# Seven products of halves in an order that changes the PSUM bank, and at the start one weight piece loaded earlier and one prepared later

## The chip, the cores and the metric

The kernel runs on one core of one Trainium2 chip. The metric is the device time of one execution in microseconds; lower is better. The kernel before takes 654.24 us (median of 4 runs, 654.07 to 654.77). Its profiled execution has a span of 652.4 us; in all profiled executions here the time is 1.7 to 2.0 us above the span.

## The reference

```python
# attention: B=4, H=8, S=768, D=48
for t in range(S):
    cur = einsum('bhd,bhe->bhde', u * k_t, v_t)
    y[:, :, t] = einsum('bhd,bhde->bhe', r_t, state + cur)
    state = w_t[..., None] * state + einsum('bhd,bhe->bhde', k_t, v_t)
x = y.transpose(0, 2, 1, 3).reshape(3072, 384)
# MLP: w_in is 384 x 2048, w_out is 2048 x 384
h = x @ w_in
g = 0.5 * h * (1 + erf(h / sqrt(2)))
out = g @ w_out
```

The two weights arrive as 64-bit floats and are converted to 32-bit floats on the chip.

## The kernel before

The tokens are worked on in eight stretches x = 0 to 7 of 384. Each needs an attention and an MLP, and the MLP of x - 1 runs interleaved with the attention of x: the MLP is a generator that is advanced step by step, and at chosen steps one attention "slot" is put in. The last MLP, x = 7, has no attention beside it.

For x > 0 two of the three blocks of 128 tokens of the second MLP product are done with seven products of half size in place of eight (sums of blocks in, sums of results out). Each product is 16 matmuls 128x192. They accumulate in two PSUM tiles of one bank each, o1/o3 in one bank (A), o2 in the other (B):

```python
o1, o2 = psum(), psum()                       # tag "mm", two buffers
product(o1, of_blocks(0, 0), of_w(0, 0), True)
nc.scalar.copy(out=p1, in_=o1)                # P1, bank A, ScalarE reads
yield
product(o1, of_blocks(0, 1), of_w(1, 0))
nc.scalar.copy(out=o_sb[0][:, 0:HM], in_=o1)  # P2, bank A
yield
product(o2, of_sums(s2), of_t(1), True)
nc.vector.tensor_add(u2, o2, p1)              # P3, bank B, VectorE reads
yield
product(o2, of_sums(s3), of_t(2))
nc.vector.tensor_add(u3, o2, p1)              # P4, bank B
for k in range(2):
    nc.vector.tensor_sub(s2[k], gs[k + 2][:, :, 0:128], s2[k])
yield
o3 = psum()
product(o3, of_sums(s1), of_t(0), True)
nc.vector.tensor_add(o_sb[1][:, HM:], o3, u3) # P5, bank A
yield
product(o2, of_blocks(1, 1), of_t(3))
nc.vector.tensor_add(o_sb[1][:, 0:HM], o2, p1)# P6, bank B
...                                           # store of o_sb[1]
yield
product(o3, of_sums(s2), of_w(1, 1))
nc.vector.tensor_add(o_sb[0][:, HM:], o3, u2) # P7, bank A
...                                           # store of o_sb[0]
```

A weight piece (16 in all) is loaded by SyncE's queue into a raw buffer, made into f and e by ScalarE (`prepare`), and into the 32-bit weight by four VectorE operations (`finish`). `conversion` of piece i first prepares piece i + 1, then finishes piece i, then loads piece i + 3:

```python
def conversion():
    i = converted[0]
    ...
    prepare(i + HALFWAY)                      # HALFWAY = 2
    if wide:
        yield from finish(pieces[i][0], raws[i], *halfway[i])
    for _ in weight_in():
        pass
```

The start, up to the first MLP, at the end of the attention of x = 0 (it runs as two units):

```python
for _ in chain(shares, weight_in(), weight_in()):  # last share of x=1, v; second and third piece
    pass
convert()                       # first piece
for unit in units[:-1]: ...     # y of one unit: ysb, its transfers, two ScalarE copies into xT
for _ in range(2): ...
piece = conversion()            # second piece; prepares the third on ScalarE
next(piece)
next(units[-1])                 # y of the other unit: two VectorE and two ScalarE copies into xT
for _ in piece:
    pass
slots = attention(1, 0)
next(slots)
keep_warm(12)                   # twelve matmuls on zeros
```

## Time and profile before

| | before |
|---|---|
| median of 4 runs | 654.24 us |
| span of the profiled run | 652.4 us |
| TensorE, VectorE, ScalarE busy | 97%, 59%, 28% |
| first MLP matmul begins | 49.53 us |
| first update of r for x = 1 (VectorE) begins | 60.87 us |
| period of the MLP blocks x = 1 to 6 | 75.4 to 75.6 us |
| waits of the products for u2 | 7 of 0.8 us |

TensorE is the bound: from about 125 us on the chain of work that ended last is only matmuls. The prediction below shows the lines on the products and on the start. One more place is needed, the time-ordered records between the first MLP matmul and the first update of r. The columns are start, duration, engine, line, operation, output and inputs, shapes, count, and in brackets the idle time before it with what ended it.

```profile
57.27 1.61 PE L315 MATMUL d<-kx,rkw_in 64*64 64x64 f32 x92
...
60.51 0.33 PE L315 MATMUL d<-kx,rkw_in 64*64 64x64 f32 x4 [1.63 <-issue]
...
60.87 1.76 DVE L350 TENSOR_TENSOR rkw_in<-rkw_in 128x1536 f32<-128x1536 f32 x1 [4.47 <-PE d L315]
```

In a group of 96 equal matmuls TensorE stops for 1.63 us after the 92nd, waiting for nothing that the profile shows ("issue"); VectorE's update of r needs the end of that group.

### The profile page before, as it was taken

How to read it: one execution, taken by the hardware profiler on the slowest of the kernel's cores; microseconds unless marked ns; L12 is line 12 of the kernel's file. 1: busy time of each engine (PE TensorE's matmuls, PEld its weight loads, DVE VectorE, ACT ScalarE, POOL GpSimd, SP SyncE). 2: the span in 40 equal slices, each digit the busy share in tenths (PEclk: the TensorE clock that was granted, in tenths of full speed). 3: DMA queues.
4: the chain of work that ended last, by engine and by line, in shares of the span. 5: the costliest groups of instructions: out<-in, count | busy, mean ns of one | idle time of the engine just before them, and what ended most of it. 6: DMA issues, size and time to landing. Idle time of an engine off the chain costs nothing.

```text
span 652.4 us, 17509 instructions
## 1 busy us (share of the span) xinstructions
PE 633.8 (97%) x7937; PEld 451.2 (69%) x7937; DVE 382.6 (59%) x718; ACT 183.9 (28%) x338; POOL 5.7 (1%) x20
## 2 busy tenths in 40 slices
PE   8898998999999999999999999999999999999997
PEld 4555665566796668866697667966688667975695
DVE  8977999756941676428761479426763378600120
ACT  2245465233302531043212432024311432122200
POOL 3000000000000000000000000000000000000000
PEclk9999999999999999999999999999999999999999
DMA  4576347115001340004101240013301000010000
GB/s 169 157 248 242 103 157 267 34 47 139 12 3 36 82 113 2 26 22 126 58 2 35 66 131 2 11 37 86 99 2 34 15 1 2 2 35 13 0 1 36
DMA packets 20409, 43.26 MB, mean 66 GB/s; under 512 B 2672, under 2 KB 6512, under 8 KB 20336
## 3 DMA queue, kind: packets, MB, share of 16 engines
q1 hardware_dynamic: 13344, 26.97, 12.1%
q10 hardware_dynamic: 6992, 15.18, 8.7%
q8 instruction: 62, 1.02, 0.6%
q14 instruction: 11, 0.09, 0.0%
HBM read 36.24 MB, written 4.72 MB: 63 GB/s over the span
## 4 chain that ended last, share of the span: by engine, by line
PE 85%; DVE 9%; issue 2%; ACT 1%; DMA 1%; ACTq 0%; SPq 0%; DVEq 0%
PE h_ps L566 35%; PE o_ps L584 20%; PE o_ps L638 14%; PE d L401 6%; PE d L315 3%; DVE rkw_in L350 2%; PE y_ps L485 2%; PE y_ps L503 2%; DVE e L264 1%; PE kv_ps L453 1%; DVE a_sb L358 1%; DMA raw<-in_w_in_dram 1%; PE kt_ps L437 1%; PE warm L167 1%; DVE w_out_sb L268 1%
## 5 line engine op out<-in xcount | busy, mean ns | idle before, releaser
L566 PE MATMUL h_ps<-xT,w_in_sb 128*128 128x384 f32 x768 | 257.4, 490 | 1.1 <-ACT xT L516 1.1
L566 PEld LDWEIGHTS h_ps<-xT,w_in_sb 128*128 128x128 f32 x768 | 143.3, 190 | 97.7 <-ACT xT L516 1.5
L568 ACT ACTIVATE g<-h_ps 128x384 f32<-128x384 f32 x128 | 62.9, 491 | 210.5 <-PE h_ps L566 210.4
L638 PE MATMUL o_ps<-w_out_sb,g 128*128 128x384 f32 x320 | 106.2, 489 | 0.0
L638 PEld LDWEIGHTS o_ps<-w_out_sb,g 128*128 128x128 f32 x320 | 59.9, 190 | 40.4 <-DVE o_sb L644 0.6
L425 DVE COPY_PREDICATED a_sb<-quarter,d 128x384 f32<-128x384 uint8 x162 | 82.6, 552 | 3.7
L584 PE MATMUL o_ps<-t,s 128*128 128x192 f32 x336 | 58.2, 330 | 3.6 <-DVE u L612 3.6
L584 PEld LDWEIGHTS o_ps<-t,s 128*128 128x128 f32 x336 | 54.3, 190 | 6.0 <-DVE u L612 5.7
L644 DVE COPY o_sb<-o_ps 128x384 f32<-128x384 f32 x10 | 5.6, 558 | 87.1 <-PE o_ps L638 87.0
L401 PEld LDWEIGHTS d<-kx,rkw_in 64*64 64x64 f32 x1728 | 36.4, 133 | 9.8 <-issue 6.5
L401 PE MATMUL d<-kx,rkw_in 64*64 64x96 f32 x1728 | 39.8, 245 | 0.0
L519 ACT COPY ysb<-y_ps 128x384 f32<-128x384 f32 x8 | 3.8, 477 | 125.7 <-PE y_ps L503 125.7
L584 PE MATMUL o_ps<-w_out_sb,g 128*128 128x192 f32 x224 | 38.8, 327 | 0.4 <-ACT p L606 0.4
L584 PEld LDWEIGHTS o_ps<-w_out_sb,g 128*128 128x128 f32 x224 | 36.6, 190 | 2.6 <-ACT p L606 0.7
L380 ACT COPY kx<-rkw_in 128x384 f32<-128x384 f32 x54 | 31.2, 645 | 24.3 <-PE d L401 20.2
L412 DVE TENSOR_TENSOR rkw_in<-rkw_in,tot_sb 128x768 f32<-128x768 f32 x18 | 17.2, 957 | 31.7 <-PE d L401 31.7
L315 PEld LDWEIGHTS d<-rkw_in 64*64 64x64 f32 x1152 | 18.7, 134 | 11.9 <-issue 5.6
L576 DVE TENSOR_TENSOR s<-g 128x512 f32<-128x512 f32 x14 | 9.6, 686 | 28.9 <-ACT g L568 28.9
L167 PE MATMUL warm<-zeros 128*128 128x512 bf16 x81 | 23.2, 408 | 2.3 <-ACT zeros L162 2.3
L516 ACT COPY xT<-y_ps 48x384 f32<-48x384 f32 x46 | 21.8, 474 | 12.5 <-issue 12.0
L315 PE MATMUL d<-rkw_in 64*64 64x64 f32 (+1 forms) x1152 | 21.3, 221 | 3.0 <-issue 1.3
L612 DVE TENSOR_TENSOR u<-o_ps,p 128x192 f32<-128x192 f32 x7 | 2.5, 358 | 35.1 <-PE o_ps L584 35.1
(80 smaller groups left out, 569.6 us busy)
## 6 DMA issues: line engine op xcount, KB each, us to landing
rkw_in<-in_rkw_dram ACTq DMA_DIRECT2D x40, 288.0 KB, 2.9
raw<-in_w_out_dram SPq DMA_DIRECT2D x8, 768.0 KB, 4.4
raw<-in_w_in_dram SPq DMA_DIRECT2D x7, 768.0 KB, 7.9
rkw_in<-in_rkw_dram SPq DMA_DIRECT2D x16, 288.0 KB, 5.8
out_dram<-o_sb SPq DMA_DIRECT2D x24, 192.0 KB, 1.9
v_in<-in_v_dram ACTq DMA_DIRECT2D x5, 584.0 KB, 3.8
v_in<-in_v_dram SPq DMA_DIRECT2D x3, 584.0 KB, 6.6
rkw_in<-in_rkw_dram SPq DMA_DIRECT2D x2, 768.0 KB, 5.8
```

What stands on the lines that cost most here:

```text
L167: nc.tensor.matmul(t, lhsT=zeros[:, 0:128], rhs=zeros, start=True, stop=True)
L315: nc.tensor.matmul(d[half[p], g, n * width:(n + 1) * width], lhsT=kc[half[g], b, i, p], rhs=right(half[g], b, i, p), start=True, stop=True)
L350: nc.vector.tensor_mul(rk, rk, tt)
L380: nc.scalar.copy(out=z, in_=r4[:, :, :, f, :])
L401: nc.tensor.matmul(d[half[p], g, i * 3 * C // 2:(i + 1) * 3 * C // 2], lhsT=kc[half[g], (n + i) // NI, (n + i) % NI, p], rhs=rx[half[g], 2 ...
L412: nc.vector.tensor_mul(z, z, t2[:, :, 1:2].to_broadcast(z.shape))
L425: nc.vector.copy_predicated(out=an[:, :, :, :, (a + 1) * h:], mask=mask.to_broadcast(data.shape), data=data)
L516: copy(out=xT[s, pair, :].rearrange("p (i c t) -> p c i t", c=2, t=C), in_=y[s])
L566: nc.tensor.matmul(h_ps, lhsT=w_in_sb[:, f // FI, j, f % FI * 128:(f % FI + 1) * 128], rhs=xT[:, j, :], start=(j == 0), stop=(j == NJ - 1))
L568: nc.scalar.activation(out=gs[group][:, f % FG], in_=h_ps, func=AF.Gelu)
L584: nc.tensor.matmul(o, lhsT=lhs(j), rhs=rhs(j), start=start and j == 0, stop=(j == HF - 1), skip_group_check=True)
L638: nc.tensor.matmul(o, lhsT=block(i, f // HF, f % HF), rhs=w_out_sb[:, f, :], start=(f == 0), stop=(f == NF - 1))
```

## The change

It has two aims: no product should follow one in the same bank whose result is still being read, and ScalarE's last copies of x should not stand behind the preparation of a weight piece. For the latter, the second piece is also loaded ahead of the last share and v.

```diff
-    def conversion():
+    def conversion(ahead=True):
...
-        prepare(i + HALFWAY)
+        if ahead:
+            prepare(i + HALFWAY)
...
             product(o2, of_sums(s2), of_t(1), True)
             nc.vector.tensor_add(u2, o2, p1)
             yield
+            o3 = psum()
+            product(o3, of_sums(s1), of_t(0), True)
+            for k in range(2):
+
+                nc.vector.tensor_sub(s2[k], gs[k + 2][:, :, 0:128], s2[k])
+            yield
             product(o2, of_sums(s3), of_t(2))
             nc.vector.tensor_add(u3, o2, p1)
-            for k in range(2):
-
-                nc.vector.tensor_sub(s2[k], gs[k + 2][:, :, 0:128], s2[k])
-            yield
-            o3 = psum()
-            product(o3, of_sums(s1), of_t(0), True)
             nc.vector.tensor_add(o_sb[1][:, HM:], o3, u3)
             yield
             product(o2, of_blocks(1, 1), of_t(3))
...
-    for _ in chain(shares, weight_in(), weight_in()):
+    for _ in chain(weight_in(), shares, weight_in()):
         pass
...
-    piece = conversion()
+    piece = conversion(ahead=False)
     next(piece)
     next(units[-1])
     for _ in piece:
         pass
+    prepare(HALFWAY + 1)
```

More of the change, by code (lines that the diff above doesn't have):

```diff
@@ L613, in mlp @@
             yield
-            product(o2, of_sums(s3), of_t(2))
-            nc.vector.tensor_add(u3, o2, p1)
+            o3 = psum()
+            product(o3, of_sums(s1), of_t(0), True)
             for k in range(2):
@@ L619, in mlp @@
             yield
-            o3 = psum()
-            product(o3, of_sums(s1), of_t(0), True)
+            product(o2, of_sums(s3), of_t(2))
+            nc.vector.tensor_add(u3, o2, p1)
             nc.vector.tensor_add(o_sb[1][:, HM:], o3, u3)
```

## The prediction

> **What bounds the kernel now.** I read the busy table first, then the list of who waited for whom, then the time-ordered records around each edited place. I call the seven products of halves by their place in the kernel before: P1, P2 (bank A, read by ScalarE), P3 (bank B, read into u2), P4 (B, read into u3), P5 (A, o3), P6 (B), P7 (A).
>
> ```profile
> PE 633.8 (97%) x7937; PEld 451.2 (69%) x7937; DVE 382.6 (59%) x718; ACT 183.9 (28%) x338; POOL 5.7 (1%) x20
> ```
>
> TensorE is busy for 97% of a span of 652.4 us, and the chain that ended last is 85% TensorE. From about 125 us on that chain is nothing but matmuls, one block of about 75.4 us per x (210.46, 286.06, 361.43 start the same group). So a microsecond in which TensorE stands still is a microsecond of the run, and time saved on another engine there is worth nothing. The list of waits names such stills:
>
> ```profile
> PEld o_ps L584 <- DVE u L612: 5.7, 7, 0.8
> PE o_ps L584 <- DVE u L612: 3.6, 7, 0.5
> ```
>
> Seven times, once for each x that uses the halves, the products wait for VectorE's u2. The time-ordered records of the block for x = 1 (start, duration, engine, line, operation):
>
> ```profile
> 182.80 2.87 PE L584 MATMUL o_ps<-t,s 128*128 128x192 f32 x16
> 185.78 0.36 DVE L612 TENSOR_TENSOR u<-o_ps,p 128x192 f32<-128x192 f32 x1 [4.86 <-PE o_ps L584]
> ...
> 186.19 5.17 PEld L584 LDWEIGHTS o_ps<-t,s 128*128 128x128 f32 x32 [0.81 <-DVE u L612]
> 186.19 5.47 PE L584 MATMUL o_ps<-t,s 128*128 128x192 f32 x32 [0.52 <-DVE u L612]
> ...
> 190.28 0.42 DVE L470 TENSOR_TENSOR st<-st,kv_ps 128x96 f32<-128x96 f32 x2
> 190.61 0.35 DVE L615 TENSOR_TENSOR u<-o_ps,p 128x192 f32<-128x192 f32 x1
> 190.88 1.28 DVE L618 TENSOR_TENSOR s<-g,s 128x512 f32<-128x512 f32 x2
> 191.59 1.63 PE L485 MATMUL y_ps<-a_sb,v_in 64*64 64x64 f32 x96
> ...
> 193.15 2.87 PE L584 MATMUL o_ps<-t,g 128*128 128x192 f32 x16
> 195.69 2.63 PEld L584 LDWEIGHTS o_ps<-w_out_sb,s 128*128 128x128 f32 x16
> 195.85 2.76 PE L584 MATMUL o_ps<-w_out_sb,s 128*128 128x192 f32 x16
> ```
>
> P3 ends at 185.67, u2 takes 185.78 to 186.14, and P4 (the first 16 of the 32 at 186.19) starts 0.05 us later. P4 to P5 and P6 to P7 change the bank and have no wait. Between P5 and P6 lie the 96 small matmuls of an attention slot (L485).
>
> The second place is the start of the first MLP:
>
> ```profile
> 45.69 0.96 ACT L516 COPY xT<-y_ps 48x384 f32<-48x384 f32 x2 [1.56 <-issue]
> ...
> 45.72 2.76 PE L167 MATMUL warm<-zeros 128*128 128x512 bf16 x12
> 45.82 1.12 DVE L516 COPY xT<-y_ps 48x384 f32<-48x384 f32 x2 [0.60 <-PE y_ps L503]
> 46.68 0.93 ACT L249 ACTIVATE f<-raw 128x768 f32<-128x768 f32 x1
> ...
> 47.50 1.00 ACT L250 ACTIVATE e<-raw,two 128x768 f32<-128x768 uint32 x1
> ...
> 48.52 0.96 ACT L516 COPY xT<-y_ps 48x384 f32<-48x384 f32 x2
> ...
> 49.53 4.14 PE L566 MATMUL h_ps<-xT,w_in_sb 128*128 128x384 f32 x12 [1.05 <-ACT xT L516]
> ```
>
> The y that the last two copies of x read is complete at 45.78, yet they start at 48.52, behind f and e of the third weight piece. TensorE has only warming matmuls until 48.48 and then waits 1.05 us.
>
> **What the Trainium skill says.** "PSUM — Partial Sum Buffer", section "PSUM bank collisions raise a hardware error": two engines must not use one bank and quadrant at once, reads by two engines included, and accesses are to be guarded by bank. The trace agrees twice: P4 starts 0.05 us after u2's read of its bank, and the built program makes ScalarE's last two copies of x wait for VectorE's two, which only read other columns of the same banks. "TensorE: Matmul & The Clock Gate", its opening table: ScalarE's and VectorE's queues are strictly first in, first out, and TensorE may pull weight loads ahead of running matmuls. The trace agrees: the ready copies sit behind f and e; P7's first weights load at 195.69, 0.16 us ahead of its matmul, while after the wait for u2 both start together at 186.19. "DMA: Bandwidth & Descriptors", section "Queues, rings and completion order": SyncE and ScalarE each own one row of rings, and descriptors of a ring are consumed in order. So a piece issued ahead of a share should land ahead of it; the trace of before has raw pieces landing in order of issue, 8.1 us after issue for the second piece.
>
> **The change, part by part.** No work is added or removed; each engine keeps the same operations. It moves four things.
>
> First, the order becomes P1 A, P2 A, P3 B, P5 A, P4 B, P6 B, P7 A. P3 is followed by P5, whose bank was freed by ScalarE's copy after P2, more than 1.5 us earlier; P4 then finds u2 read 2 us ago. What the wait costs: P7 starts 2.60 us after P6 in the last x (633.27 to 635.87), so 2.60 is a product without a wait. There P3 starts at 624.68 and P4 at 627.97, 3.29 later, and P4's first matmul is shown 0.10 early because it came with its weights (627.97 to 633.27 is 5.30 for two products instead of 5.20). So the wait costs 3.29 + 0.10 - 2.60 = 0.79 us, the same as the weight loads' idle of 0.81. It goes six times. The seventh, the last x, has no attention slot between P4 and P6; there P6 must wait for u3 in bank B, a read of the same 0.36 us: minus 0.79, plus 0.79. Sum: 6 x 0.79 = 4.7 us.
>
> For x = 1 to 6, P6 now leans on u3, which stands in VectorE's line behind the state update and the two subtractions. In the block above: state done at 190.70, subtractions 190.61 to 191.89 (1.28), u3 from 191.80 to 192.16 (0.36), P6 allowed at 192.21 (0.05). TensorE, 0.79 us earlier, would begin P6 at 193.15 - 0.79 = 192.36. It fits by 0.15 us: no wait, but hardly any room.
>
> Second and third, f and e of the third piece (0.93 + 1.00) go behind the last copies. These then start not at 45.78 but when VectorE's pair is done, 46.94, and end at 46.98 + 0.96 = 47.94. TensorE finishes its twelfth warming matmul some 0.2 us after the eleventh; 12 x 0.213 from 45.72 lets the first MLP matmul in at about 48.28. So the start moves from 49.53 to 48.3: 1.2 us. ScalarE's next work, f and e, then kx, shifts to about 47.95 to 52.0, against 51.65 for the end of kx before; VectorE wants that f at 50.47 and the first gelu is not needed before 53.
>
> Fourth, the second piece is loaded ahead of the last share of r, k, w and of v, 288 + 584 KB. Near 40 us the queues moved 350 to 390 GB/s, so it lands about 2.4 us before 41.93, near 39.5. ScalarE's f, e then end near 41.3 instead of 43.76, so ysb and its six transfers leave 2 us earlier. Nothing in the end waits on that alone: their rows queue behind the fourth piece on the same ring (landing about 46.4) and should be there near 47.4, before 47.94. It is what makes the second part possible, because before the transfers landed only near 49.
>
> Does 1.2 us survive? From 49.53 to 60.87 the chain is TensorE, and VectorE stands idle for 4.47 us before the first update of r at 60.87, waiting for it. From there to 108.4 VectorE is busy 46.79 of 47.53 us, TensorE 46.93; both start from that same point and move together. So it survives. One piece can grow: TensorE stands still 1.63 us at 58.88 in the middle of a group of equal matmuls, waiting for nothing the profile shows, while the DMA engines are 94% busy. I take it for a late fetch of instructions; three loads now start about 2.4 us earlier, so this queue should be shorter then. I count 0.4 us for it, a guess between 0 and 1.6.
>
> Sum: 4.7 + 1.2 + 0.4 = 6.3 us; 654.4 - 6.3 = 648.1 us.
>
> **The rivals.** One: P6's wait for u3 takes the place of P4's wait for u2. For it: the margin is only 0.15 us, and in the last x it certainly happens. Against it: the slot's 1.56 us lie between. If u3 were 0.3 us late each time, 1.0 us comes back (some 649 us); if the slot hid nothing, all 4.7 (653). Two: the earlier start at 48.3 is lost, because the rows of x from the transfers land late, or VectorE's conversions bound that stage. For it: VectorE at 98% from 60.87 on; against: its 4.47 us idle just before. The result would be near 649.5. Three: the stall of 1.63 us goes away altogether or doubles: 646.9 or 650.1.
>
> **Range and chances.** The first part is arithmetic on a repeated block and sure to about 1 us; the start is sure to about 1 us on either side and the stall adds another. I take 646.3 to 650.2. Two per cent is 13 us, more than twice everything the change touches, so "within 2%" is nearly certain.
>
> **What would show it.** Right: the waits of o_ps for u of L612 gone, one wait for u3 left (in the last x); blocks of 74.6 instead of 75.4 us; P6 starting right behind the slot; the first MLP matmul near 48.3, released by the warming matmuls or ScalarE's copy; the update of r near 59.3. Wrong: six waits of P6 on u3; an update of r still near 60.9; a longer unexplained stall near 58; ScalarE's f of the second piece still at 42.

## The result, and the profile after

The changed kernel takes 647.25 us (median of 4 runs, 646.92 to 648.42) against 654.24. The ratio is 0.9895, with a 95% interval of 0.9878 to 0.9912. A ratio here is the mean time of one kernel's fast runs over that of the other's of the same rounds, so it is not quite the ratio of the medians. The change is under 2%, as forecast.

The busy table, the first line of its page, and the only two waits of the products for VectorE in the list of waits (engine and line, what it waited for, total us, times, longest):

```profile
PE 629.8 (98%) x7918; PEld 451.5 (70%) x7937; DVE 382.1 (59%) x718; ACT 183.4 (28%) x338; POOL 5.6 (1%) x20
```

```profile
PEld o_ps L585 <- DVE u L622: 0.7, 1, 0.7
PE o_ps L585 <- DVE u L622: 0.5, 1, 0.5
```

The seven waits for u2 are gone and one for u3 is there, in the last x. The time-ordered records of the block for x = 1:

```profile
180.91 8.07 PE L585 MATMUL o_ps<-t,s 128*128 128x192 f32 x48
183.88 0.36 DVE L613 TENSOR_TENSOR u<-o_ps,p 128x192 f32<-128x192 f32 x1 [4.85 <-PE o_ps L585]
...
188.71 1.28 DVE L619 TENSOR_TENSOR s<-g,s 128x512 f32<-128x512 f32 x2
188.90 1.63 PE L486 MATMUL y_ps<-a_sb,v_in 64*64 64x64 f32 x96
189.92 0.35 DVE L622 TENSOR_TENSOR u<-o_ps,p 128x192 f32<-128x192 f32 x1
...
190.46 2.87 PE L585 MATMUL o_ps<-t,g 128*128 128x192 f32 x16
```

P3, P5 and P4 are now one unbroken group of 48 matmuls, three times 2.60 us and the 0.27 us by which the record of a lone product of 16 (2.87) also exceeds 2.60. u3 ends at 190.27, and P6 starts at 190.46 right behind the 96 small matmuls of the slot, without a wait.

The start, from the same view:

```profile
43.77 0.96 ACT L517 COPY xT<-y_ps 48x384 f32<-48x384 f32 x2 [1.57 <-issue]
45.45 2.77 PE L167 MATMUL warm<-zeros 128*128 128x512 bf16 x11
45.58 1.11 DVE L517 COPY xT<-y_ps 48x384 f32<-48x384 f32 x2
46.78 0.96 ACT L517 COPY xT<-y_ps 48x384 f32<-48x384 f32 x2 [2.06 <-DVE xT L517]
47.76 0.93 ACT L250 ACTIVATE f<-raw 128x768 f32<-128x768 f32 x1
48.14 3.52 PEld L567 LDWEIGHTS h_ps<-xT,w_in_sb 128*128 128x128 f32 x12 [0.41 <-ACT xT L517]
48.17 4.11 PE L567 MATMUL h_ps<-xT,w_in_sb 128*128 128x384 f32 x12
...
58.62 0.33 PE L316 MATMUL d<-kx,rkw_in 64*64 64x64 f32 x4 [1.14 <-issue]
...
58.99 1.76 DVE L351 TENSOR_TENSOR rkw_in<-rkw_in 128x1536 f32<-128x1536 f32 x1 [2.85 <-PE d L316]
```

ScalarE's last copies now wait for VectorE's pair, and no longer stand behind f and e. The first MLP matmul has no wait in brackets, but its weight load has one. In five profiles with the early load, of runs that follow below (e2, e5, e7, e10, e12), this matmul starts 2.60 us behind the first warming matmul, to the hundredth; I take that for "released by the warming matmuls". Here it is 2.72 (45.45 to 48.17). The last of the transfers of x's rows landed at 47.92 (read from the packed trace: issued at 44.13, 3.79 us), 0.25 us ahead of the matmul. So in this execution the transfers set the start, 0.12 us later than the warming matmuls would have. Where the 6.7 us of the span went can be read off by setting the same groups of the chain that ended last side by side (the first two rows are from the time-ordered records):

| group starts at | before | after | difference |
|---|---|---|---|
| first MLP matmul | 49.53 | 48.17 | 1.36 |
| first update of r for x = 1 | 60.87 | 58.99 | 1.88 |
| second-product group of x = 0 (28 matmuls) | 113.51 | 111.61 | 1.90 |
| last-block group (32 matmuls), x = 1 | 199.94 | 197.25 | 2.69 |
| x = 2 | 275.54 | 272.07 | 3.47 |
| x = 3 | 350.92 | 346.65 | 4.27 |
| x = 4 | 426.52 | 421.47 | 5.05 |
| x = 5 | 501.89 | 496.06 | 5.83 |
| x = 6 | 577.49 | 570.87 | 6.62 |
| x = 7 | 638.64 | 631.95 | 6.69 |

The start gives 1.90 us (0.24 of it because y came earlier in this execution, 45.58 against 45.82), each of the six blocks 0.78 to 0.80 (4.72 together), the last x 0.07.

### The profile page after: what moved, and what is told of

Same layout as the page of the kernel before. It is cut to its first block, busy times and chain, and to the rows that moved or that the text cites. A ratio compares the mean times of both kernels' runs of the same rounds, so it can differ in the third digit from the quotient of the medians.

```text
span 645.7 us, 17490 instructions
## 1 busy us (share of the span) xinstructions
PE 629.8 (98%) x7918; PEld 451.5 (70%) x7937; DVE 382.1 (59%) x718; ACT 183.4 (28%) x338; POOL 5.6 (1%) x20
## 3 DMA queue, kind: packets, MB, share of 16 engines
q8 instruction: 62, 1.02, 0.7%
HBM read 36.24 MB, written 4.72 MB: 63 GB/s over the span
## 4 chain that ended last, share of the span: by engine, by line
PE 87%; DVE 9%; issue 2%; DMA 1%; ACT 1%; SPq 0%; DVEq 0%
PE h_ps L567 35%; PE o_ps L585 20%; PE o_ps L639 14%; PE d L402 6%; PE d L316 3%; DVE rkw_in L351 2%; PE y_ps L504 2%; PE y_ps L486 2%; PE kv_ps L454 2%; DVE e L265 1%; PE kt_ps L438 1%; PE warm L167 1%; DVE a_sb L359 1%; DMA rkw_in<-in_rkw_dram 1%; DVE w_out_sb L269 1%
## 5 line engine op out<-in xcount | busy, mean ns | idle before, releaser
L585 PE MATMUL o_ps<-t,s 128*128 128x192 f32 x336 | 56.4, 328 | 0.0
L167 PE MATMUL warm<-zeros 128*128 128x512 bf16 x62 | 20.7, 421 | 2.7 <-ACT zeros L162 2.3
```

Source lines behind the costliest of these rows:

```text
L167: nc.tensor.matmul(t, lhsT=zeros[:, 0:128], rhs=zeros, start=True, stop=True)
L585: nc.tensor.matmul(o, lhsT=lhs(j), rhs=rhs(j), start=start and j == 0, stop=(j == HF - 1), skip_group_check=True)
```

## The experiments

Twelve runs were made, of ten kernels, in three sessions. The times of a kernel scatter by one to three us in these sessions (before: 652.59 to 656.26), so effects of about 1 us are read from stages within a profile, and the times say whether the whole agrees.

A part of this scatter has a visible sign. Each execution comes with its mean granted TensorE clock, and it is either 0.999 to 1.000 or 0.996 to 0.997. In the two profiled executions of the second kind (e1, e4 again) the clock is at half for some 3 us near the start; from e1:

```profile
52.00:54.00 2.00, 2.00 (x4) 1.01 (x3) 0.12 (x1) 0.44 (x2) 0.00 (x0) 0.50 1.03 398
```

(a stretch, busy us and count of each engine, then the clock, 0.50.) There the twelve matmuls of a group take 5.83 us in place of 4.1. In e1's session six of before's eleven executions had the low clock and averaged 655.03 us, the other five 653.16. Over the three sessions it came in 19 of 46 executions with the load order of before, and in 3 of 42 with the early load. So part of what the early load gains in the times goes with the dip being rarer. No run was made to say why, and the split was made only after the runs; below, "full clock" means the executions at 0.999 or more alone.

The start needs a further care: VectorE's copies of y begin anywhere from 44.15 to 46.31 us, in kernels whose program up to there is the same but for one moved load, so the absolute time of the first MLP matmul says little. I use the distance from those copies to the first MLP matmul, the distance from there to the update of r, and the stall in between. All from the time-ordered records:

| kernel | VectorE's copies | to first MLP matmul | from there to update of r | stall |
|---|---|---|---|---|
| before | 45.82 | 3.71 | 11.34 | 1.63 |
| changed | 45.58 | 2.59 | 10.82 | 1.14 |
| e1, order alone | 44.47 | 5.50 | 11.13 | none; half clock |
| e2, start alone | 45.95 | 2.48 | 11.02 | 1.41 |
| e3, early load alone | 45.97 | 2.50 | 11.11 | 1.42 |
| e3 again | 45.80 | 2.60 | 11.09 | 1.41 |
| e4, late preparation alone | 44.44 | 3.68 | 11.10 | 1.42 |
| e4 again | 44.15 | 3.89 | 11.64 | 1.96 |
| e5, late u3 | 46.09 | 2.50 | 11.37 | 1.76 |
| e6, same bank | 45.85 | 3.42 | 11.91 | 2.23 |
| e7, last x alternating | 44.76 | 2.50 | 11.09 | 1.48 |
| e10, four loads left out | 45.77 | 2.48 | 9.32 | none |
| e11, two loads held | 45.45 | 2.66 | 9.40 | none |
| e12, e7 and e11 | 46.31 | 2.49 | 9.33 | none |

### e1_order_only and e2_start_only: each part alone

e1 is the kernel before with the third hunk of the diff alone; e2 is the changed kernel with that hunk taken back.

> Only the order of the products is changed, the start is that of the kernel before. Theory (each part earns its own time, in its own stage): the six waits for u2 go, 6 x 0.79 = 4.7 us, so about 649.5 us against 654.2, with the first MLP matmul still at 49.5 us and the update of r at 60.9 us of the span. Rival (the two parts lean on each other): anything from 647.3, if the order alone gave all, to 652, if part of the gain needs the early start.

> Both start changes, the order of the products of before. Theory: 1.36 us from the first MLP matmul (49.53 to 48.17) and 0.5 us from the shorter stall of TensorE near 57, 1.9 us in all, so about 652.3 us, with the seven waits for u2 of 0.79 us each still there. Rival: less than 1 us, if VectorE's conversions take the early start back.

Measured: e1 649.26 us, ratio 0.9926 (0.9906 to 0.9946); e2 652.34 us, ratio 0.9974 (0.9954 to 0.9994). Both as the theory said, and their product, 0.9900, is near the 0.9895 of both. e1's list of waits has the one wait for u3, e2's still the seven for u2. The parts add and lie in different stages. At full clock e1 gains 4.25 us (0.7 either way), near the 4.7 of the blocks, but e2 only 0.6 (1.0 either way): that its ratio came out as expected is partly due to the dips of before, and the 0.5 us expected of the stall is not borne out (see below). e1's start was not quite that of before, although the program is:

```profile
49.97 5.83 PE L566 MATMUL h_ps<-xT,w_in_sb 128*128 128x384 f32 x12 [2.85 <-ACT xT L516]
```

y came early (44.47), the copies behind f and e still ended at 49.92, and the clock dip followed.

### e3_load_only and e4_prepare_only, each run twice: which edit of the start does it

```diff
# e3: kernel before, with only
-    for _ in chain(shares, weight_in(), weight_in()):
+    for _ in chain(weight_in(), shares, weight_in()):
# e4: kernel before, with only conversion(ahead=False) and prepare(HALFWAY + 1)
```

> Only the second weight piece loaded ahead of the last share; the third piece is still prepared between the copies of x. Theory: with the early load ScalarE is done with its first pair of copies at about 44.7 us and has 2 us to spare before VectorE's pair ends at 46.7; f and e (about 1.9 us) fit into that hole, so the last copies start at about 46.8 all the same and the first MLP matmul at 48.2: the same gain as both start changes, about 652.3 us. Rival (the author's: f and e have to go behind the copies): the last copies wait for f and e, the MLP starts at 49 or later, 653.5 to 654.2 us.

> Only the third piece prepared behind the last copies; the load order of before. Theory: ScalarE's last copies end at about 47.9 us, but ysb is still made late (43.7), so the transfers of x's rows land only near 49 and hold the first MLP matmul there: a gain of 0.3 to 0.6 us, about 653.8 us. Rival: the copies alone set the start, 48.2 us, and this change alone gives 1.4 to 1.9 us, about 652.5 us.

> A repetition of the early load alone, in a fresh session, to tell it from the third piece's move alone, which is repeated beside it. Theory: the first MLP matmul 2.5 us behind the time at which VectorE starts its copies of y (3.7 before), 0.3% under before (ratio 0.996 to 0.998).

> A repetition of the third piece's move alone. The first run left it open: the profile had the first MLP matmul at 48.1 us (49.5 before), though 3.7 us behind the start of VectorE's copies as before, and the times showed nothing (ratio 0.9991, interval 0.9971 to 1.0011). If the move alone helps, the ratio is 0.997 to 0.998; if the late ysb holds the start, 0.999 to 1.000 and the first MLP matmul 3.3 us or more behind VectorE's copies or released by the transfers.

Measured: e3 652.12 us, ratio 0.9961 (0.9936 to 0.9986), again 653.14, 0.9977 (0.9961 to 0.9994). e4 653.72 us, 0.9991 (0.9971 to 1.0011), again 653.41, 0.9985 (0.9972 to 0.9999). The records of e3, first run:

```profile
44.78 0.94 ACT L249 ACTIVATE f<-raw 128x768 f32<-128x768 f32 x1
45.60 0.99 ACT L250 ACTIVATE e<-raw,two 128x768 f32<-128x768 uint32 x1
45.97 1.12 DVE L516 COPY xT<-y_ps 48x384 f32<-48x384 f32 x2
47.18 0.96 ACT L516 COPY xT<-y_ps 48x384 f32<-48x384 f32 x2 [0.59 <-DVE xT L516]
48.47 4.11 PE L566 MATMUL h_ps<-xT,w_in_sb 128*128 128x384 f32 x12
```

f and e still stand before the last copies and cost nothing: ScalarE is through with them at 46.59 and waits another 0.59 us for VectorE. With the early load the distance to the first MLP matmul is 2.5 to 2.6 us whether f and e go before or behind. (It is longer, 3.42, in e6 alone, where the transfers landed late.) So moving the preparation was not needed once the load is early. At full clock e3 gains 1.3 and 1.4 us, each with an interval of 1.4 to 1.5 either way.

Alone the move does little in the times (at full clock 0.1 and 0.9 us, from three and two executions), and the distance stays at 3.7 to 3.9 us. But y was early in both profiles, and e1, the one profile of the old start with as early a y, has 5.50. Against e1 the move gains 1.6 to 1.8 us, against before nothing; what it is worth by itself depends on when y comes. In the second run of e4 the release is named:

```profile
48.04 2.17 PE L567 MATMUL h_ps<-xT,w_in_sb 128*128 128x384 f32 x6 [1.24 <-DMA xT<-ysb]
```

The transfers of x's rows, made late, hold it: the last landed at 47.79, 0.25 us before. In the first run the record names ScalarE's copies, which end at 47.89, but the last transfer landed at 47.87 and the matmul again starts 0.25 us behind it, at 48.12; behind a copy that releases it, it starts after 0.05 (49.48 to 49.53 in before, 49.92 to 49.97 in e1). The same 0.25 us (0.24 once) stands in seven profiles: both of e3, both of e4, e6, e11 and the changed kernel. e4 ran with an early y both times, so what it would do with a late one is not shown, and whether its 0.1% is more than nothing stays open.

### e5_late_u3: how much room P6 has

```diff
                 nc.vector.tensor_sub(s2[k], gs[k + 2][:, :, 0:128], s2[k])
+            nc.vector.tensor_add(s1[0], gs[0][:, :, 128:256], gs[2][:, :, 128:256])
             yield
             product(o2, of_sums(s3), of_t(2))
```

> The changed kernel with one more VectorE operation of 128x512 (0.61 us from start to start in the trace), a sum of s1 that is made again with the same result, ahead of u3. It measures the room that the sixth product has before u3's read holds it. Theory: u3 ends 0.14 us before TensorE wants the bank, so 0.61 us of delay shows as 0.47 us in each of six blocks, 2.8 us in all, about 650.1 us, and the waits list shows six waits for u3 besides the last x's. Rival: there is more room than the trace lets one read (over 0.6 us), and the time stays at 647.3 us.

Measured: 649.61 us, ratio 0.9930 (0.9913 to 0.9946). Only half of what was expected of the blocks came: three of the six grew, by 0.46 us each (for x = 3 from 74.58 to 75.04, from one last-block group to the next), 1.4 us in all; the other three kept their 74.8. The remaining difference of its span to the changed kernel's (648.0 against 645.7) is the start, whose stall was long in this execution. First a block that waits, then one that does not:

```profile
191.48 0.35 DVE L623 TENSOR_TENSOR u<-o_ps,p 128x192 f32<-128x192 f32 x1
191.88 2.87 PE L585 MATMUL o_ps<-t,g 128*128 128x192 f32 x16 [0.39 <-DVE u L623]
...
266.07 0.35 DVE L623 TENSOR_TENSOR u<-o_ps,p 128x192 f32<-128x192 f32 x1
266.47 2.87 PE L585 MATMUL o_ps<-t,g 128*128 128x192 f32 x16
```

An attention that starts a sequence (even x) updates six states in place of five, about 0.4 us more of VectorE work ahead of u3. In the changed kernel P6 has 0.14 us of room beside such an attention (190.46 against 190.27 + 0.05) and 0.60 beside the others (265.05 against 264.05 + 0.35 + 0.05). I had read one block and taken it for all six. The mechanism holds: 0.61 - 0.14 = 0.47 and 0.61 - 0.60 = 0.01.

### e6_same_bank: the bank or the order

```diff
-            o1, o2 = psum(), psum()
+            o1 = psum()
+            both = ps.tile([128, BANK], F32, name="o_ps", tag="mm", bufs=2)
+            o2, o3 = both[:, 0:HM], both[:, HM:2 * HM]
...
-            o3 = psum()
-            product(o3, of_sums(s1), of_t(0), True)
+            product(o3, of_sums(s1), of_t(0))
```

> The order of the changed kernel, but o3 lies in the other columns of o2's bank (its first product starts without clearing, as P3 has cleared the bank). Theory (it is the change of the bank that removes the wait, not the order): P5 waits for u2 again, 0.79 us in all seven x, and P7 for the read after P6, another 0.79 us in all seven, and in the last x P6 waits 0.4 us more: 11.5 us, about 658.7 us. Rival (the order is what counts, or only the columns touched): 647.3 us with no new waits.

Measured: correct, 659.09 us, ratio 1.0081 (1.0063 to 1.0099). From its list of waits:

```profile
PEld o_ps L585 <- DVE u L615: 5.7, 7, 0.8
PEld o_ps L585 <- DVE o_sb L627: 5.2, 7, 0.7
```

The order is the changed one, and the waits are back: for u2 ahead of P5 and for the read after P6 ahead of P7. The first six blocks are each 1.50 us longer than the changed kernel's, 9.0 together, and the last x 1.9. So the order alone does not remove the wait; o3 must lie in another bank than o2, and the program guards more than the columns that are touched. In this run o2 and o3 are also one tile, so it does not tell a guard by bank from a guard by tile. (The guard is in the built program: the semaphore waits name those reads. No run here tells what an unguarded access would do.)

### e7_last_alternating: the last x

Without slots between them, all seven products of the last x can change the bank. The edit puts P3 ahead of P2 and P4 ahead of P5 there.

```diff
+            if x == NX - 1:
+                product(o2, of_sums(s2), of_t(1), True)   # P3 ahead of P2
+                nc.vector.tensor_add(u2, o2, p1)
+                yield
             product(o1, of_blocks(0, 1), of_w(1, 0))
...                                                       # P5 likewise behind P4
```

> The changed kernel, but in the last x, which has no attention slots between the products, the order is P1 A, P3 B, P2 A, P4 B, P5 A, P6 B, P7 A, so that every product changes the bank. Theory: there the waits for p1 (P2 3.27 us behind P1 instead of 2.60: 0.67 us) and for u3 (P6 0.71 us late) go, 1.4 us in all, about 645.9 us. Rival: the end of the program is bound by something else (the last store, VectorE's sums that P3 needs early), under 0.5 us.

Measured: 646.70 us, ratio 0.9885 (0.9868 to 0.9902), too close to 0.9895 to tell apart. In the profile no product of halves waits for VectorE or ScalarE any more, and from the last x's first h_ps to its last group it takes 49.16 us (580.72 to 629.88) where the changed kernel takes 50.56 (581.39 to 631.95): 1.40 us, as expected.

### e10_light and e11_held_loads: the stall near 57 us

e10 gives a wrong result: pieces six to nine are not loaded. e11 is right: it only holds the eighth and ninth load back.

```diff
# e10
+            if 5 <= len(raws) <= 8:
+                raws.append(raws[len(raws) - 5])
+                return
# e11, with weight_in(held=i in (4, 5)) in conversion
+            if held:
+                nc.vector.memset(dst[:, 0].bitcast(U32)[:, 0:1], 0)
             if not gate:
                 nc.sync.dma_start(out=dst, in_=src)
```

> WRONG RESULT ON PURPOSE: the changed kernel without four of its weight loads (pieces six to nine use the data of the first four), so that the DMA engines are nearly idle from about 52 us on. It tells what TensorE's stall of 1.14 us (1.63 before) near 57 us is. Theory (a block of instructions that is fetched late because the DMA rings are full of weights): the stall falls to 0.3 us or less, the update of r comes near 58.1 us instead of 59.0, and the time is about 0.9 us lower, 646.4 us. Rival (the stall has to do with the matmuls or another engine): it stays at 1.1 us and the time at 647.3 us.

> The changed kernel, with the eighth and ninth weight loads held back until VectorE has gone past the conversions of the fifth and sixth piece (a memset of one column in front of each), so that the DMA engines have less to do from 53 to 60 us. Right result. Theory (TensorE's stall near 57 us is a late fetch of instructions behind weight packets): the stall of 1.1 to 2.2 us seen in every run with the full loads goes as it did when four loads were left out, the first update of r comes about 9.4 us behind the first MLP matmul instead of 10.8 to 11.9, two memsets cost 0.14 us on VectorE; together 1.2 us less than the changed kernel, about 646 us in a session where before takes 654.2. Rival one: the held pieces come too late for ScalarE and what is gained is lost again before the first o_ps products (which then start not earlier than about 63.4 us behind the first MLP matmul). Rival two: it was something else that went with the four loads, and the stall stays.

Measured: e10 646.94 us, ratio 0.9894 (0.9877 to 0.9912); e11 646.34 us, 0.9877 (0.9858 to 0.9895). In both profiles the stall is gone, and the update of r comes 9.32 and 9.40 us behind the first MLP matmul. In e11 the 96 matmuls are one group:

```profile
55.81 1.63 PE L318 MATMUL d<-kx,rkw_in 64*64 64x64 f32 x96
...
57.51 1.76 DVE L353 TENSOR_TENSOR rkw_in<-rkw_in 128x1536 f32<-128x1536 f32 x1 [1.48 <-PE d L318]
```

The share of the DMA engines' time from 48 to 59 us was 0.94 in before, 0.89 in changed, 0.50 in e11, 0.12 in e10. So the stall goes when the DMA engines have less to do there. Their load alone does not make it: e1 has the share at 0.87 and no stall. What tells all fourteen profiles apart is one packet of 16 KiB of the instruction queue (read from the packed trace). The stall is always behind the 92nd matmul of this group. In the ten profiles that have it, the 93rd starts 1.21 to 1.49 us behind the end of that packet (before: end 59.08, matmul 60.51; changed: 57.29, 58.62). In the four that have none it starts 1.54 to 2.52 us behind it: the packet is there in time. In e10, e11 and e12 it starts 5.6 to 6.1 us behind the first MLP matmul in place of 8.2 to 9.1; in e1 it starts after 7.5, and the group itself comes 1.7 us late because of the half clock. So a late block of instructions fits every profile. No record names the packet as the release, and why it starts earlier with fewer weights under way is argued, so the last step is not shown. e10's times did not show its shorter stage, which is within the scatter; e11's did, by 1.2 us against the changed kernel's ratio, though the intervals overlap. The rival that the held pieces come too late is out: the second-product group starts 62.03 us behind the first MLP matmul (110.14 - 48.11), 63.44 in changed.

### e12_both

> The held loads and the alternating banks of the last x together. Theory: they lie in different stages and add: 1.2 + 1.4 = 2.6 us less than the changed kernel, about 644.6 us where before takes 654.2, ratio about 0.985; in the profile the stage from the last x's first h_ps to its last o_ps takes 49.2 us instead of 50.6, and the stretch from the first MLP matmul to the update of r about 9.4 us. Rival: under 1 us in all, if the runs scatter about something that neither touches.

Measured: 645.47 us, ratio 0.9863 (0.9847 to 0.9878), the lowest of all. The stages are as expected (9.33 us to the update of r, 49.16 us in the last x). The gain over the changed kernel is 0.0032 x 654 = 2.1 us by the ratios, 2.6 expected. It is faster than before; the intervals of e12 and of the changed kernel, which ran in different sessions, just touch at 0.9878.

## Why the prediction was right, point by point

The time on record was 648.1 us, the median 647.25, inside the range. The mechanism of the order was right, that of the start nearly so; that the sum came so close is partly luck, in the stall.

**The order.** Right in size and place: 6 x 0.79 predicted, 4.72 read from the blocks, and e6 shows that sharing the bank brings the waits back. The last x was put at minus 0.79 plus 0.79; it gave 0.07, as the new wait costs 0.72. The room of P6 was worked out as 0.15 us and is 0.14, but only beside an attention of even x; e5 shows 0.60 beside the others. The first rival, P6 held by u3, did not come about outside the last x.

**The start.** The 1.2 us from 49.53 to 48.3 is right (2.5 to 2.6 us behind VectorE's copies in place of 3.7). Its bound, the warming matmuls, is right for five profiles with the early load. In the changed kernel's own it was the transfers, by 0.12 us: the prediction had their rows landing near 47.4 with nothing waiting on them, and they landed at 47.92. What the prediction said of the parts is right in one half: the early load makes it possible. It missed that the early load alone is enough, because f and e then fit ahead of VectorE's pair (e3). It said that the transfers landed only near 49 in the order of before; they did in before (49.04), and in both runs of e4 they hold TensorE until 48.0 to 48.1, so the mechanism stands with another number. With the early load they still held it by 0.76 us once, in e6.

**It survives.** 1.88 us at the update of r are 1.90 at the second-product group of x = 0 and are still there at the end. The second rival is out.

**The stall.** The 0.4 us counted for it is the one step that the runs do not bear out as an effect of the change. The profile gave 0.49 (1.63 to 1.14), but in the seven profiles with the early load and all loads it is 1.14 to 2.23, mean 1.55; without the early load it is 1.63, 1.42, 1.96 and, in e1, nothing. Three loads that start about 2 us earlier do not shorten it beyond its scatter, so it is luck that 0.4 was counted and 0.49 found. The guess of a late fetch fits all fourteen profiles, and e11 and e12, with loads held back, are without the stall and 1.4 to 1.5 us shorter there.

## What to carry to other kernels

When two accumulations use different banks, put a product of the other bank between a product and the next one in its own bank, so that the read of a result lies beside matmuls; then check what room the moved read has, in every kind of block. Before moving work behind a copy, see whether an earlier load would let it end before the copy is due at all. And a stall that waits for "issue" in the middle of equal instructions while the DMA engines are full is worth one try with loads held back. Look at the clock of each execution, too, before a difference of 1 us in the times is put down to the change.

## What the Trainium skill lacked or had wrong

- "Runtime: NRT & Kernel Launch", section "Instruction fetch mechanics", says that crossing a 16 KiB block costs little and is mostly hidden. The sizes agree (62 packets, 1.02 MB on the instruction queue of before), but TensorE stood still for 1.14 to 2.23 us at one place in ten profiles, and each time went on 1.21 to 1.49 us behind the end of one instruction packet; it did not in the three whose loads there were left out or held, nor in e1. That the fetch is the cause fits all of them, but no record names it.
- "PSUM — Partial Sum Buffer", section "PSUM bank collisions raise a hardware error", gives the rule to guard a bank but not its price. Here a product of 16 matmuls that must wait for a VectorE read of 128x192 in its bank started 0.79 us late: 0.36 us is the read itself.
- "TensorE: Matmul & The Clock Gate", Part 3, "What overlaps and what doesn't", says that a weight load overlaps a running matmul only when its row group differs. Here all loads of a product are full 128x128 ones, of the same rows, and they are busy for 2.57 to 2.63 us in the 2.60 us that a product of 16 takes from start to start (P6 and P7 in before), so they must overlap its matmuls; the ends of matmuls, which are modelled, are not needed for this.
- No page that I read says how long the fetch of a core's instructions can be held up by its own data loads: the stall of 1.14 us went when the DMA share from 48 to 59 us fell from 0.89 to 0.50.
